# Attention and soft mixture of experts on one core: the attention output is no longer formed

## The chip, the cores and the metric

One core of a Trainium2 chip runs the whole program. The metric is device time in microseconds, from 2 runs of the kernel before.

## The reference

Attention with pooled keys comes first, then a soft mixture of experts over its output. Values are the keys. There are 4 batches of 12288 queries and 768 keys of 128 channels, and 32 slots (8 experts with 4 each).

```
kv_pool = kv.reshape(B, H // r, r, W // r, r, C).mean(axis=(2, 4))
k = v = kv_pool.reshape(B, -1, C) @ w_sr
s = scale * (q @ k.transpose(0, 2, 1))
a = np.exp(s - s.max(-1, keepdims=True))
x = ((a / a.sum(-1, keepdims=True)) @ v).reshape(B * N, C)
logits = x @ phi
d = softmax of logits over all queries (axis 0)
slot_input = d.T @ x
slot_out = for each expert: relu(slot_input @ w1) @ w2
c = softmax of logits over the slots (axis 1)
return c @ slot_out
```

The softmax over axis 0 spans all 49152 queries, so no output can be written before the last query's logits are known.

## The kernel before

All work is declared as steps for a planner (class Plan) that keeps a clock for each engine, knows a cost for each step and which buffers are free, and emits the instructions of PE, VectorE, ScalarE and GpSimd in the order that it finds. Priorities come from due times (T0 = HEAD + i * PER for block i).

The unit is a block of 512 queries (96 blocks). Scores are kept with the keys on the partitions: `qk` (L473 to L475) makes three products of 512 columns for each of 6 key tiles, with q and the keys split into a high and a low part. The maximum over the keys lies across partitions, so it takes several steps: `rowmax1` (L480) reduces with a transpose in 32x32 blocks, `rowmax2` and `rowmax_pe` (L500) bring the partition quarters together through PE, `rowmax4` (L510) transposes back and spreads it. `sub` (L518) takes the maximum from the scores on VectorE, `exp_hi` and `exp_t` (L525, L529) compute the exponential twice on ScalarE, and `plo` (L534) makes the low part of P on GpSimd.

`av_hi` and `av_lo` (L551, L552, L559) form the attention output: P is the stationary side, the values with a column of ones and the projected values (161 columns) stream, 72 products in a block. So output, sum and logits of 128 queries come out together. Every four blocks a group (`g0` to `g7a`) normalises the logits, keeps a running maximum over the queries, and adds D.T @ x to `acc` (L690: 16 fp32 products of 32 output columns in four column positions of the array).

After the last group come the slot inputs (`t_psi`, L1020), the experts (L1040, L1063), and the output: `o_mm` (L1120) multiplies the combine weights, in four row positions of the array, with the slot outputs; ScalarE and VectorE evict (L1127, L1129), SyncE's queue writes. At the head the keys of batch 0 are summed on VectorE as they land (L309 to L313), first 512 of the 768 keys and then the rest; later batches are summed by DMA.

PSUM is divided in advance: three pairs of banks for scores, two single banks for all else.

Of the kernel before, what the change touches and what calls it, by code (L numbers as in the profile page):

```python
# [11 lines left out]
F16 = mybir.dt.float16  # L12
U32 = mybir.dt.uint32
# [6 lines left out]
P = 128  # L20
EPS = 1e-9
PK = 16.0
KSPLIT = 512
VK = 4096.0
Q32 = 32


AVD = 2.0
HOLD = 0.7
URGE = 60.0  # L30


class Plan:
# [4 lines left out]

    LAG = 0.08

    def __init__(self, rings):
        self.cap = rings
        self.ops = []
        self.users = {}
        self.bank = 0

    def op(self, eng, cost, lat, prio, deps, fn, acq=(), use=(), at=0.0, slack=0.0, hot=False, raw=0.0):
        n = len(self.ops)
        if eng != "PE" and any(ring == "m" for ring, _ in use):
            prio -= URGE  # L50
        for key in list(acq) + list(use):
            self.users.setdefault(key, []).append(n)
        self.ops.append((eng, cost, lat, prio, list(deps), fn, list(acq), at, slack, hot, raw, list(use)))
        return n

    def emit(self):
        ops = self.ops
        inf = math.inf
        done = [None] * len(ops)
# [7 lines left out]
        for n, o in enumerate(ops):  # L67
            avail.setdefault(o[0], [])
            if waits[n] == 0:
                ready[n] = o[7]  # L70
                avail[o[0]].append(n)
        left = {key: len(u) for key, u in self.users.items()}
        sums = {key: sum(ops[n][0] == "PE" for n in u) for key, u in self.users.items()}
        summed = {}
# [3 lines left out]
        banks = [None] * self.cap["m"]  # L78
        tops = [None] * self.cap["m"]
        where = {}  # L80
        free = dict.fromkeys(avail, 0.0)
        todo = len(ops)

# [3 lines left out]
        def bank(key):  # L87
            found = []
            for b in range(len(banks)):
                if key[0] == "pq":  # L90
                    t = gone(banks[b])
                    beside = banks[b] is not None and banks[b][1][0] == "px" and t == inf
                    if beside:
                        t = summed.get(banks[b], inf)
                    found.append((max(t, gone(tops[b])), not beside, b))
                else:
                    found.append((max(gone(banks[b]), gone(tops[b])), False, b))
            return min(found)

        def acquire(n, now):  # L100
            t = 0.0
            for key in ops[n][6]:
                ring = key[0]
                if ring == "m":
                    t = max(t, bank(key[1])[0])
                    continue
                cap = self.cap.get(ring)
                held = rings.get(ring, ())
                if cap is not None and len(held) >= cap:
                    t = max(t, gone(held[-cap]))  # L110
            if ops[n][0] == "ACT":
                for key in ops[n][11]:
                    if key[0] == "m" and key[1][0] == "px":
                        t = max(t, gone(tops[where[key]]))
            return None if t == inf else t

        def best(e):
            found = []
            for n in avail[e]:
                t = acquire(n, free[e])  # L120
                if t is not None:
                    found.append((max(free[e], ready[n], t), ops[n][3], n))
            if not found:
                return None
            t0 = min(found)[0] + 0.12
            hot = [f for f in found if ops[f[2]][9]]
            if hot:
                h = min(hot)
                if h[0] - t0 < HOLD:
                    fits = [(p, t, n) for t, p, n in found if t <= t0 and t + ops[n][1] <= h[0] + 0.1]  # L130
                    return min(fits) if fits else (h[1], h[0], h[2])
            return min((p, t, n) for t, p, n in found if t <= t0)

        while todo:
            picks = [(c[1], e, c[2]) for e in avail if (c := best(e)) is not None]
            if not picks:
                held = {k: left[k] for k in left if left[k] and left[k] < len(self.users[k])}
# [1097 lines left out]
```

## Time and profile before

| | us |
|---|---|
| median of 2 runs | 1114.07 (1114.04 to 1114.10) |
| span of the profiled execution | 1112.4 |
| PE busy | 1046.7 (94%) |
| VectorE busy | 984.9 (89%) |
| GpSimd busy | 866.2 (78%) |
| ScalarE busy | 822.7 (74%) |

The profile is of one execution, and its span runs from the first to the last instruction; 1.7 us lie between it and the median. Matmuls are pipelined, so busy time of PE counts the time in which a product drains, and a group's mean duration is longer than the step from one product to the next. The granted clock of PE averages 0.975 of full speed.

### The profile page before, as it was taken

How to read it: one execution, taken by the hardware profiler on the slowest of the kernel's cores; microseconds unless marked ns; L12 is line 12 of the kernel's file. 1: busy time of each engine (PE TensorE's matmuls, PEld its weight loads, DVE VectorE, ACT ScalarE, POOL GpSimd, SP SyncE). 2: the span in 40 equal slices, each digit the busy share in tenths (PEclk: the TensorE clock that was granted, in tenths of full speed). 3: DMA queues.
4: the chain of work that ended last, by engine and by line, in shares of the span. 5: the costliest groups of instructions: out<-in, count | busy, mean ns of one | idle time of the engine just before them, and what ended most of it. 6: DMA issues, size and time to landing. Idle time of an engine off the chain costs nothing.

```text
span 1112.4 us, 24632 instructions
## 1 busy us (share of the span) xinstructions
PE 1046.7 (94%) x10198; PEld 897.3 (81%) x10198; DVE 984.9 (89%) x1492; ACT 822.7 (74%) x1006; POOL 866.2 (78%) x480
## 2 busy tenths in 40 slices
PE   3699999999999999999999999999999999997876
PEld 2588888888888888888888888888888888886343
DVE  7899889889889989899899988989989988987895
ACT  1677778778778778878877788688788777875563
POOL 0579897788899888789889889779889889773340
PEclk9799999999999999999999999999999999999885
DMA  9315421111125310120136210120110110113398
GB/s 342 117 22 132 96 44 39 39 58 39 39 54 124 91 42 22 39 70 27 39 83 123 71 53 1 39 96 2 39 39 1 39 39 2 39 39 115 141 407 360
DMA packets 17407, 89.15 MB, mean 80 GB/s; under 512 B 1680, under 2 KB 3984, under 8 KB 11152
## 3 DMA queue, kind: packets, MB, share of 16 engines
q1 hardware_dynamic: 13408, 69.47, 16.8%
q0 software_dynamic: 3312, 17.70, 8.4%
q8 instruction: 81, 1.33, 0.5%
q10 hardware_dynamic: 576, 0.41, 0.1%
q14 instruction: 30, 0.25, 0.1%
HBM read 58.87 MB, written 25.17 MB: 76 GB/s over the span
## 4 chain that ended last, share of the span: by engine, by line
PE 67%; DVE 27%; issue 2%; ACT 2%; POOL 1%; DMA 1%; SPq 0%; DVEq 0%; ACTq 0%; POOLq 0%
PE m L551 11%; PE m L552 10%; PE m L559 10%; PE s L473 9%; PE s L475 9%; PE s L474 9%; DVE t L518 8%; DVE r L480 8%; PE m L500 3%; PE m L690 2%; DVE mb L510 2%; PE po L1120 2%; DVE o L1129 2%; DVE cm L628 1%; DVE pool L311 1%
## 5 line engine op out<-in xcount | busy, mean ns | idle before, releaser
L534 POOL TENSOR_TENSOR plo<-t,phi 128x1536 f16<-128x1536 f32 x190 | 595.8, 3143 | 125.1 <-ACT t L529 123.8
L525 ACT ACTIVATE phi<-t,lnk 128x1536 f16<-128x1536 f32 x192 | 301.6, 1571 | 133.5 <-DVE t L518 132.9
L480 DVE TRANSPOSE_TENSOR_REDUCE r<-s 128x32 f32<-128x1024 f32 x288 | 349.8, 1236 | 27.1 <-PE s L475 21.1
L551 PE MATMUL m<-vhi,phi 128*128 128x161 f16 x2280 | 354.5, 234 | 2.5 <-DVE m L505 1.3
L552 PE MATMUL m<-vlo,phi 128*128 128x160 f16 x2280 | 353.5, 233 | 0.0
L518 DVE TENSOR_TENSOR t<-s,mb 128x1024 f32<-128x1024 f32 (+1 forms) x384 | 342.9, 949 | 8.8 <-DVE mb L510 0.9
L529 ACT ACTIVATE t<-t,lnk 128x1536 f32<-128x1536 f32 x192 | 299.8, 1568 | 2.3
L551 PEld LDWEIGHTS <-phi 128*128 128x128 f16 x2304 | 227.0, 99 | 22.9 <-issue 22.8
L473 PE MATMUL s<-qhi,khi 128*128 128x512 f32 x576 | 238.1, 413 | 6.5 <-DVE t L518 6.1
L552 PEld LDWEIGHTS <-phi 128*128 128x128 f16 x2304 | 225.5, 98 | 5.2 <-issue 3.3
L475 PE MATMUL s<-qhi,klo 128*128 128x512 f32 x576 | 227.2, 394 | 0.0
L474 PE MATMUL s<-qlo,khi 128*128 128x512 f32 x576 | 226.6, 393 | 0.0
L559 PE MATMUL m<-vhi,plo 128*128 128x161 f16 x2280 | 221.9, 233 | 0.3 <-POOL plo L534 0.3
L559 PEld LDWEIGHTS <-plo 128*128 128x128 f16 x2304 | 174.8, 100 | 1.3 <-issue 0.6
L463 POOL TENSOR_TENSOR qlo<-q,qhi 128x512 fp32r<-128x512 f32 x96 | 125.7, 1310 | 26.9 <-ACT qhi L459 26.9
L569 ACT ACTIVATE xl<-m 128x322 f32<-128x322 f32 x189 | 81.0, 428 | 76.1 <-PE m L559 75.7
L473 PEld LDWEIGHTS s<-qhi,khi 128*128 128x128 f32 x576 | 109.7, 190 | 29.9 <-issue 3.6
L475 PEld LDWEIGHTS s<-qhi,klo 128*128 128x128 f32 x576 | 109.2, 190 | 24.6 <-DVE klo L353 0.5
L474 PEld LDWEIGHTS s<-qlo,khi 128*128 128x128 f32 x576 | 109.8, 191 | 20.3 <-issue 0.7
L510 DVE STREAM_TRANSPOSE mb<-m 128x512 f32<-128x512 f32 x96 | 68.3, 711 | 3.3
L459 ACT ACTIVATE qhi<-q 128x512 fp32r<-128x512 f32 x96 | 59.2, 617 | 2.4 <-issue 1.0
L505 DVE TENSOR_REDUCE m<-m 128x16 f32<-128x64 f32 x96 | 21.5, 224 | 40.5 <-PE m L500 40.5
(140 smaller groups left out, 854.1 us busy)
## 6 DMA issues: line engine op xcount, KB each, us to landing
q<-qT SPq DMA_DIRECT2D x23, 1024.0 KB, 4.8
outT<-o SPq DMA_DIRECT2D x21, 1024.0 KB, 5.2
kva<-kvT POOLq DMA_DIRECT2D x9, 1536.0 KB, 11.4
kva<-kvT SPq DMA_DIRECT2D x3, 1536.0 KB, 10.5
kv<-kv SPq DMA_DIRECT2D x8, 512.0 KB, 5.7
w<-w SPq DMA_DIRECT2D x2, 1536.0 KB, 6.4
w<-w SPq DMA_DIRECT2D x4, 768.0 KB, 4.6
outT<-o SPq DMA_DIRECT2D x6, 512.0 KB, 4.3
```

Source lines behind the costliest of these rows:

```text
L463: nc.gpsimd.tensor_tensor(out=lo, in0=q_src(i), in1=hi.bitcast(F32), op=ALU.subtract)
L473: nc.tensor.matmul(s, khi[:, ks], hi, start=True, stop=False)
L474: nc.tensor.matmul(s, khi[:, ks], lo, start=False, stop=False)
L475: nc.tensor.matmul(s, klo[:, ks], hi, start=False, stop=True)
L480: nc.vector.tensor_reduce(out=MX[i][:, 2 * u : 2 * u + 2, :].rearrange("p t b -> p (t b)"), in_=S[i, u].rearrange("p t (b j) -> p (t b) j" ...
L518: nc.vector.tensor_tensor(out=TT_[i, h][:, o : o + n, :], in0=S[i, t // 2][:, u : u + n, :], in1=MX[i].unsqueeze(1).broadcast_to([P, n, BQ ...
L525: nc.scalar.activation(hi, TT_[i, h], AF.Exp, bias=lnk, scale=SCALE)
L529: nc.scalar.activation(t, t, AF.Exp, bias=lnk, scale=SCALE)
L534: eng.tensor_tensor(out=lo, in0=TT_.pop((i, h)), in1=PP[i, h], op=ALU.subtract)
L551: nc.tensor.matmul(px, p, vhi[:, t, :], start=(t == 0), stop=False)
L552: nc.tensor.matmul(px[:, 1:], p, vlo[:, t, :], start=False, stop=False)
L559: nc.tensor.matmul(px, PP[i, t // TH][1][:, t % TH, ks], vhi[:, t, :], start=False, stop=(t == NT - 1))
```

## The change

The program is written anew around another order of the same algebra. Its unit is a tile of 128 queries (384 tiles), its group eight tiles (48 groups).

- Scores have the queries on the partitions: `qk` multiplies a tile's q, as the stationary side, with all keys, six products of 384 columns into one slot of two PSUM banks. `rowmax` is then one reduction along a row, and `exp` one ScalarE instruction from PSUM with the maximum as its bias and the row's sum as a second result. P stays fp32.
- `turn` transposes P of two tiles in 32x32 blocks on VectorE. Keys then lie within each partition quarter, with 24 key blocks apart.
- `kv_u_mm` and `kv_u_out` multiply the pooled keys with w_sr @ phi. `l_mm` makes the logits as turned P times that: 96 fp32 products of 32 rows, 32 output columns and 256 columns for a group, in 16 positions of the array, into four banks. `l_ev`, `l_sum` and `l_turn` fold the 16 parts together.
- The attention output is not formed. `a_mm` multiplies D with P (32 slots by 768 keys), `a_ev`, `a_sc` and `a_add` keep that sum through a batch, and only at a batch's end `b_t` and `b_mm` multiply it with the values.
- PSUM is four slots of two banks, handed out by the planner to whatever step asks. The planner now picks by earliest start plus a weight times a due time from a table (DUE). Half of the combine weights (3.1 MB) are written to memory and read back at the end (`k_out`, `c_load`).
- The keys of batch 0 come in one piece of 768. The output goes out in chunks of three quads of tiles instead of four.

```diff
--- before.py
+++ after.py
-AVD = 2.0
-HOLD = 0.7
-URGE = 60.0
+NSLOT = 4
+DUE = {
...
         def best(e):
             found = []
             for n in avail[e]:
-                t = acquire(n, free[e])
-                if t is not None:
-                    found.append((max(free[e], ready[n], t), ops[n][3], n))
-            if not found:
-                return None
-            t0 = min(found)[0] + 0.12
-            hot = [f for f in found if ops[f[2]][9]]
-            if hot:
-                h = min(hot)
-                if h[0] - t0 < HOLD:
-                    fits = [(p, t, n) for t, p, n in found if t <= t0 and t + ops[n][1] <= h[0] + 0.1]
-                    return min(fits) if fits else (h[1], h[0], h[2])
-            return min((p, t, n) for t, p, n in found if t <= t0)
+                t = acquire(n)
+                if t < inf:
+                    t = max(free[e], ready[n], t)
+                    found.append((t + self.PULL * ops[n][3], t, n))
+            return min(found) if found else None
 
         while todo:
...
+    slot = [pm.tile([P, 2, 512], F32, tag=f"s{k}", name=f"s{k}") for k in range(NSLOT)]
...
+    def kv_u_mm(b):
+        for h in range(2):
+            nc.tensor.matmul(sl("pu", b)[:, h, :HK], wu_sb, pooled[b][:, h * HK : (h + 1) * HK], start=True, stop=True)
+
+    def kv_u_out(b):
+        U4[b] = bp.tile([P, NBL, NS], F32, tag="u4", name=f"u4_{b}")
+        nc.vector.transpose(out=halves(U4[b].rearrange("p b s -> p (b s)")), in_=sl("pu", b)[:, :, :HK])
...
-    def qk(i, t):
-        khi, klo = kT[i // BPB]
-        hi, lo = qsp[i]
-        if t % 2 == 0:
-            S[i, t // 2] = ps.tile([P, 2, BQ], F32, tag=f"s{t // 2}", name=f"s_{i}_{t // 2}")
-        s = S[i, t // 2][:, t % 2, :]
-        ks = slice(t * P, (t + 1) * P)
-        nc.tensor.matmul(s, khi[:, ks], hi, start=True, stop=False)
-        nc.tensor.matmul(s, khi[:, ks], lo, start=False, stop=False)
-        nc.tensor.matmul(s, klo[:, ks], hi, start=False, stop=True)
-
-    def rowmax1(i, u):
+    def qk(n):
+        khi, klo = kT[n // TPB]
+        i, o = divmod(n, TB)
+        hi, lo = (a[:, o * P : (o + 1) * P] for a in qsp[i])
+        s = sl("S", n)
+        for k, (a, b) in enumerate(((hi, khi), (hi, klo), (lo, khi))):
+            for h in range(2):
+                nc.tensor.matmul(s[:, h, :HK], a, b[:, h * HK : (h + 1) * HK], start=(k == 0), stop=(k == 2))
+
+    def rowmax(n):
+        g, o = divmod(n, GT)
+        if o == 0:
+            NM[g] = gp.tile([P, GT], F32, tag="nm", name=f"nm_{g}", bufs=3)
+            RS[g] = gp.tile([P, GT], F32, tag="rs", name=f"rs_{g}", bufs=4)
+        nc.vector.tensor_reduce(out=NM[g][:, o : o + 1], in_=sl("S", n)[:, :, :HK], axis=XY, op=ALU.max, negate=True)
+
+    def exp(n):
+        g, o = divmod(n, GT)
+        if n % 2 == 0:
+            PB[n // 2] = pp.tile([P, 2, NK], F32, tag="P", name=f"P_{n // 2}", bufs=PR)
+        nc.scalar.activation(
+            halves(PB[n // 2][:, n % 2, :]), sl("S", n)[:, :, :HK], AF.Exp, bias=NM[g][:, o : o + 1], accum_out=RS[g][:, o : o + 1]
+        )
+
+    def turn(m):
+        g, o = divmod(2 * m, GT)
+        if o == 0:
+            PT[g] = pp.tile([P, NBL, GT, Q32], F32, tag="PT", name=f"PT_{g}", bufs=2)
+        nc.vector.transpose(
+            out=PT[g][:, :, o : o + 2, :].rearrange("p b t j -> p t b j"), in_=PB[m].rearrange("p t (b j) -> p t b j", j=Q32)
+        )
+
+
+    def l_mm(g):
...
+    def l_mm(g):
+        two = [sl("L", g, 0), sl("L", g, 1)]
+        u = U4[g // GPB]
+        for b in range(NBL):
+            c = b % NQD
+            for r in range(NQD):
+                rows = slice(r * Q32, (r + 1) * Q32)
+                nc.tensor.matmul(
+                    two[r // 2][c * NS : (c + 1) * NS, r % 2, : GT * Q32], u[rows, b, :],
+                    PT[g][rows, b, :, :].rearrange("p t j -> p (t j)"), start=(b < NQD), stop=(b >= NBL - NQD),
+                )
+
...
-    def rowmax2(i):
-        top = banks[plan.bank][:, 512 - (NQD + 1) * NBK :]
...
-    def rowmax_pe(i):
-        pqv = PQ.pop(i)
-        nc.tensor.matmul(pqv, sel, MX[i].rearrange("p k b -> p (k b)"), start=True, stop=True)
-        MX[i] = pqv
...
-    def rowmax4(i):
-        m = sp.tile([P, BQ], F32, tag="mb", name=f"mb_{i}", bufs=1)
-        nc.vector.transpose(out=m, in_=MX[i].unsqueeze(2).broadcast_to([P, NBK, Q32]))
...
-    def sub(i, t, n):
...
-    def exp_hi(i, h):
-        hi = PP[i, h] = sp.tile([P, TH, BQ], F16, tag="phi", name=f"phi_{i}_{h}", bufs=PB)
-        nc.scalar.activation(hi, TT_[i, h], AF.Exp, bias=lnk, scale=SCALE)
...
-    def exp_t(i, h):
-        t = TT_[i, h]
-        nc.scalar.activation(t, t, AF.Exp, bias=lnk, scale=SCALE)
...
-    def plo(i, h):
-        lo = sp.tile([P, TH, BQ], F16, tag="plo", name=f"plo_{i}_{h}", bufs=PB)
-        eng = nc.vector if i == NB - 1 else nc.gpsimd
-        eng.tensor_tensor(out=lo, in0=TT_.pop((i, h)), in1=PP[i, h], op=ALU.subtract)
-        PP[i, h] = (PP[i, h], lo)
...
-    def av_hi(i, k):
-        _, vhi, vlo = VU[i // BPB]
-        px = av_tile(i, k)
-        ks = slice(k * P, (k + 1) * P)
-        for t in range(NT):
-            p = PP[i, t // TH][0][:, t % TH, ks]
-            nc.tensor.matmul(px, p, vhi[:, t, :], start=(t == 0), stop=False)
-            nc.tensor.matmul(px[:, 1:], p, vlo[:, t, :], start=False, stop=False)
-
...
-    def av_lo(i, k):
-        vhi = VU[i // BPB][1]
-        px = PX[i, k // 2][:, k % 2, :]
-        ks = slice(k * P, (k + 1) * P)
-        for t in range(NT):
-            nc.tensor.matmul(px, PP[i, t // TH][1][:, t % TH, ks], vhi[:, t, :], start=False, stop=(t == NT - 1))
-
...
+    def l_sum(g):
+        for r in range(NQD):
+            nc.tensor.matmul(sl("x", g)[r * NS : (r + 1) * NS, 0, : GT * Q32], sel1, G[g]["LT"][:, r, :], start=True, stop=True)
+
+    def l_turn(g):
+        lq = G[g]["lq"] = gp.tile([P, GT, NS], F32, tag="lq", name=f"lq_{g}")
+        nc.vector.transpose(out=lq.rearrange("p t j -> p (t j)"), in_=sl("x", g)[:, 0, : GT * Q32])
...
+    def a_mm(g):
+        pd = sl("A", g)
+        d = G[g]["D"]
+        for k0 in range(0, GT, NQD):
+            for h in range(2):
+                for k in range(k0, k0 + NQD):
+                    c = k % NQD
+                    nc.tensor.matmul(
+                        pd[c * NS : (c + 1) * NS, h, :HK], d[:, k, :], PB[(g * GT + k) // 2][:, k % 2, h * HK : (h + 1) * HK],
+                        start=(k < NQD), stop=(k >= GT - NQD),
+                    )
+
+    def a_ev(g):
+        if g % GPB:
+            t = G[g]["ae"] = gp.tile([P, NK], F32, tag="ae", name=f"ae_{g}", bufs=1)
+        else:
+            t = acc
+        nc.scalar.activation(halves(t), sl("A", g)[:, :, :HK], AF.Copy)
+
+    def a_sc(g):
+        nc.scalar.activation(acc, acc, AF.Copy, scale=G[g]["al"])
+
+    def a_add(g):
+        nc.gpsimd.tensor_tensor(out=acc, in0=acc, in1=G[g]["ae"], op=ALU.add)
+
+    def b_t(b):
+        for k in range(NT):
+            nc.tensor.matmul(sl("bt", b)[:, 0, k * NS : (k + 1) * NS], acc[:, k * P : (k + 1) * P], sel1, start=True, stop=True)
+
+    def b_te(b):
+        AT[b] = gp.tile([P, NT, NS], F32, tag="at", name=f"at_{b}", bufs=1)
+        nc.scalar.activation(AT[b].rearrange("p k s -> p (k s)"), sl("bt", b)[:, 0, : NT * NS], AF.Copy)
+
+    def b_mm(b):
+        for k in range(NQD):
+            ks = [j for j in range(NT) if j % NQD == k]
+            for j in ks:
+                nc.tensor.matmul(
+                    sl("bx", b)[k * NS : (k + 1) * NS, 0, :VW], AT[b][:, j, :], V[b][:, j, :], start=(j == ks[0]), stop=(j == ks[-1])
+                )
+
+    def b_x(b):
+        px = sl("bx", b)[:, 0, :VW]
+        if b == 0:
+            nc.vector.tensor_copy(xacc, px)
+        else:
+            nc.vector.tensor_tensor(out=xacc, in0=xacc, in1=px, op=ALU.add)
```

PE in the steady stage. Before, the end of one block's value products, the maximum's product, and a group's update (m is a PSUM bank, rq the maxima, xl the evicted outputs):

```order
L551 LDWEIGHTS phi_1_11842
L551 MATMUL m_113<-vhi_10049,phi_1_11842 128x161
L552 LDWEIGHTS phi_1_11842
L552 MATMUL m_113<-vlo_10050,phi_1_11842 128x160
L500 MATMUL m_112<-rq_12018,sel 128x64
L559 LDWEIGHTS plo_0_11836
L559 MATMUL m_113<-vhi_10049,plo_0_11836 128x161
...
L690 MATMUL m_112<-xl_11205,D_11952 32x129 x16
```

PE now, from one tile's scores to the next tile's across a group's update and logits (s is a PSUM slot, P and PT the exponentials and the turned ones, u the projected keys):

```order
L353 MATMUL s_104<-khi_1894,qhi_2928 128x384 x2
L353 MATMUL s_104<-klo_1895,qhi_2928 128x384 x2
L353 MATMUL s_104<-khi_1894,qlo_2929 128x384 x2
L490 MATMUL s_101<-P_2649,D_3118 32x384 x2
...
L490 MATMUL s_101<-P_2858,D_3118 32x384 x2
L386 MATMUL s_102<-PT_3034,u_1_2088 32x256 x2
L386 MATMUL s_103<-PT_3034,u_1_2088 32x256 x2
...
L353 MATMUL s_104<-khi_1894,qhi_3141 128x384 x2
```

The value products have gone. A group's update stands directly ahead of another group's logits, and with them three of the four slots are taken between two tiles' scores.

VectorE in the steady stage. Before, one block from its first reduction to its last subtraction (r, m and mb are stages of the maximum, t the scores less it):

```order
L480 TENSOR_REDUCE r_50_7124<-s_0_7107 128x32
L480 TENSOR_REDUCE r_50_7124<-s_1_7119 128x32
L606 RECIPROCAL r_7155<-xl_6647 128x16
L480 TENSOR_REDUCE r_50_7124<-s_2_7130 128x32
L490 TENSOR_REDUCE m_112<-r_50_7124 128x16
L492 TENSOR_TENSOR rq_7180<-m_112,quad 128x64
L505 TENSOR_REDUCE m_50_7193<-m_112 128x16
L510 STREAM_TRANSPOSE mb_7195<-m_50_7193 128x512
L518 TENSOR_TENSOR t_0_7216<-s_0_7107,mb_7195 128x1024
```

VectorE now, a stretch of a group (nm is the maxima, lq and cm stages of the logits, klo the next batch's keys):

```order
L413 RECIPROCAL rs_4352<-rs_4352 128x8
L360 TENSOR_REDUCE nm_4595<-s_103 128x1
L402 STREAM_TRANSPOSE lq_4795<-s_104 128x256
L360 TENSOR_REDUCE nm_4595<-s_101 128x1
L429 TENSOR_REDUCE cm_4806<-ll_4798 128x8
...
L360 TENSOR_REDUCE nm_4835<-s_104 128x1
L374 STREAM_TRANSPOSE PT_4755<-P_4821 128x2x24x32
L478 TENSOR_REDUCE al_4899<-da_4840 128x1
L533 TENSOR_REDUCE RM<-ll_4556 128x8
L360 TENSOR_REDUCE nm_4835<-s_102 128x1
L374 STREAM_TRANSPOSE PT_5002<-P_4851 128x2x24x32
L374 STREAM_TRANSPOSE PT_5002<-P_4889 128x2x24x32
```

A tile leaves VectorE one maximum and half a turn; the subtractions and the stages of the maximum are gone, and the group's small steps stand between them.

## Rows read from the trace of the kernel before

**Rows 1.** Busy time by stage: length, busy us of each engine (records), granted clock, DMA share, GB/s.

```profile
120.00:900.00 780.00, 770.60 (x7697) 679.09 (x7696) 706.14 (x1044) 614.23 (x734) 674.81 (x364) 1.00 0.19 50
...
1042.00:1112.40 70.40, 49.42 (x382) 28.45 (x381) 54.95 (x87) 39.88 (x66) 18.75 (x19) 0.75 0.88 358
```

**Rows 2.** Groups by form, PE, 120 to 900 us: xcount, busy us, mean ns, idle before.

```profile
L500 PE MATMUL m<-rq,sel 128*128 128x64 f32 x152 | 31.8, 290 | 7.1 <-DVE rq L492 6.6
...
L690 PE MATMUL m<-xl,D 128*32 128x129 f32 x608 | 20.7, 275 | 0.0
```

**Rows 3.** Timeline, PE, about 400 to 406 us: start, length, line, operation, count.

```profile
400.32 0.58 PE L559 MATMUL m<-vhi,plo 128*128 128x161 f16 x6
400.89 1.09 PE L690 MATMUL m<-xl,D 128*32 128x129 f32 x32
401.91 0.24 PE L551 MATMUL m<-vhi,phi 128*128 128x161 f16 x1
...
405.17 0.39 PE L473 MATMUL s<-qhi,khi 128*128 128x512 f32 x1
405.40 0.39 PE L474 MATMUL s<-qlo,khi 128*128 128x512 f32 x1
```

**Rows 4.** Timeline, PE, 400.85 to 400.99 us alone.

```profile
400.89 0.32 PE L690 MATMUL m<-xl,D 128*32 128x129 f32 x4
```

**Rows 5.** Timeline, PE, in the tail.

```profile
1037.18 2.78 PE L1063 MATMUL pso<-w,hT 128*32 128x512 f32 x24
...
1045.24 0.50 PE L1120 MATMUL po<-chi,shi 32*128 32x512 f32 x4 [0.53 <-ACT o L1127]
1045.57 0.40 PE L1120 MATMUL po<-clo,shi 32*128 32x512 f32 x4
```

**Rows 6.** Groups by form, whole run.

```profile
L480 DVE TRANSPOSE_TENSOR_REDUCE r<-s 128x32 f32<-128x1024 f32 x288 | 349.8, 1236 | 27.1 <-PE s L475 21.1
...
L518 DVE TENSOR_TENSOR t<-s,mb 128x1024 f32<-128x1024 f32 x192 | 233.9, 1218 | 8.8 <-DVE mb L510 0.9
...
L518 DVE TENSOR_TENSOR t<-s,mb 128x512 f32<-128x512 f32 x192 | 122.7, 680 | 0.0
...
L510 DVE STREAM_TRANSPOSE mb<-m 128x512 f32<-128x512 f32 x96 | 68.3, 711 | 3.3
...
L715 DVE TENSOR_REDUCE RM<-LL 128x16 f32<-128x512 f32 x23 | 14.5, 651 | 0.0
...
L1063 PE MATMUL pso<-w,hT 128*32 128x512 f32 x32 | 3.8, 598 | 0.0
```

**Rows 7.** Timeline, VectorE, a block's subtractions and maxima in the tail.

```profile
412.38 3.55 DVE L518 TENSOR_TENSOR t<-s,mb 128x1024 f32<-128x1024 f32 x4
...
1028.09 1.86 DVE L715 TENSOR_REDUCE RM<-LL 128x16 f32<-128x512 f32 x3
```

**Rows 8.** Groups by form, ScalarE and GpSimd, whole run.

```profile
L525 ACT ACTIVATE phi<-t,lnk 128x1536 f16<-128x1536 f32 x192 | 301.6, 1571 | 133.5 <-DVE t L518 132.9
...
L1127 ACT ACTIVATE o<-po 128x1024 f32<-128x1024 f32 x23 | 23.6, 1025 | 19.1 <-PE po L1120 10.9 <-issue 5.5 <-ACT RM L720 1.6
...
L463 POOL TENSOR_TENSOR qlo<-q,qhi 128x512 fp32r<-128x512 f32 x96 | 125.7, 1310 | 26.9 <-ACT qhi L459 26.9
```

**Rows 9.** Timeline of the head, PE and VectorE.

```profile
17.85 2.08 PE L344 MATMUL m<-pooled,w_sb 128*128 128x512 f32 x2 [8.92 <-DVE pooled L313]
...
21.12 0.83 PE L473 MATMUL s<-qhi,khi 128*128 128x512 f32 x1
...
24.09 0.42 DVE L313 TENSOR_TENSOR pooled<-pool 128x256 f32<-128x256 f32 x1
```

**Rows 10.** Timeline of the tail, PE: last scores, slot inputs, first output.

```profile
1000.72 0.39 PE L475 MATMUL s<-qhi,klo 128*128 128x512 f32 x1
...
1026.42 0.64 PE L1020 MATMUL m<-sel,acc 128*128 128x32 f32 x2 [0.61 <-DVE acc L696]
...
1042.94 0.71 PE L1120 MATMUL po<-chi,shi 32*128 32x512 f32 x4
```

More of the change, by code (lines that the diff above doesn't have):

```diff
@@ L69, in emit @@
             if waits[n] == 0:
-                ready[n] = o[7]
+                ready[n] = o[8]
                 avail[o[0]].append(n)
         left = {key: len(u) for key, u in self.users.items()}
-        sums = {key: sum(ops[n][0] == "PE" for n in u) for key, u in self.users.items()}
-        summed = {}
         part = {}
@@ L77, in emit, with acquire @@
         rings = {}
-        banks = [None] * self.cap["m"]
-        tops = [None] * self.cap["m"]
-        where = {}
+        slots = [None] * NSLOT
         free = dict.fromkeys(avail, 0.0)
         todo = len(ops)
+        self.log = []
         def gone(key):
             return 0.0 if key is None else freed.get(key, inf)
[L87 to L100, printed above, removed]
+        def acquire(n):
             t = 0.0
+            need = [key for key in ops[n][6] if key[0] == "s"]
+            if need:
+                t = sorted(gone(s) for s in slots)[len(need) - 1]
             for key in ops[n][6]:
                 ring = key[0]
-                if ring == "m":
-                    t = max(t, bank(key[1])[0])
+                if ring == "s":
                     continue
-                cap = self.cap.get(ring)
+                cap = self.cap[ring]
                 held = rings.get(ring, ())
-                if cap is not None and len(held) >= cap:
+                if len(held) >= cap:
                     t = max(t, gone(held[-cap]))
[L111 to L115, printed above, removed]
+            return t
         def best(e):
@@ L136, in emit @@
             if not picks:
[L137 to L138 removed]
+                raise RuntimeError("the plan is stuck: " + str([(e, [(ops[n][3], ops[n][6]) for n in avail[e]][:8]) for e in avail]))
             t, e, n = min(picks)
[L140 removed]
+            eng, cost, lat, due, deps, fn, acq, use = ops[n][:8]
             avail[e].remove(n)
             free[e] = t + cost
[L143 removed]
+            end = t + cost + lat
             todo -= 1
             for key in acq:
[L146 to L149 removed]
+                if key[0] == "s":
+                    k = min(range(NSLOT), key=lambda i: (gone(slots[i]), i))
+                    slots[k] = key
+                    self.where[key] = k
                 else:
                     rings.setdefault(key[0], []).append(key)
[L152 removed]
+            for key in acq + use:
                 left[key] -= 1
                 part[key] = max(part.get(key, 0.0), end)
[L155 to L158 removed]
                 if left[key] == 0:
```

1050 lines of the change are left out of this document (369 added, 681 removed), and 4 rows, old and new, of the table DUE.

## The prediction

> **What bounds the kernel now.** I read the stage table first. From 120 to 900 us PE is busy 770.6 of 780.0 us, VectorE 706.1, GpSimd 674.8, ScalarE 614.2 [rows 1], and what PE still waits for in that stage is 6.6 us for the operand of the maximum's product [rows 2]. So PE sets the pace there, and an engine that is merely relieved gains nothing. The maximum's product leaves two records for each block of 512 queries; 152 of them are 76 blocks [rows 2], so a block takes 780/76 = 10.26 us, and 1024 queries take 20.5.
>
> The second reading is how much of that is product work. A key product of 512 columns starts 0.23 us after the one before it, and six value products take 0.58 us of which the last one's own 0.23 is drain, so 0.07 each [rows 3]. A block has 18 of the first (4.14), 72 of the second (5.04), the maximum's product (0.27) and a quarter of a state update of 1.09 (0.27): 9.72, with the next batch's keys 9.9. That is 96.5% of 10.26. The rest is drain and short waits that the busy share hides. I use this 96.5% below as what a bound engine reaches under a planned order.
>
> **PE after the change, for a group of eight tiles (1024 queries).** Key products: 48 of 384 columns. At 0.23 for 512, a column costs 0.45 ns, so 0.172 each, 8.3 us. The value products (10 us for as many queries) and the product for the maximum go.
>
> The logits (L386) are 96 fp32 products of 256 columns with 32 rows and 32 output columns. An fp32 product runs as two records: 16 calls of L690 leave 32 [rows 3]. Do positions run side by side? Four records of L690, in the four column positions, take 0.32 us, where one alone takes 0.27 [rows 2, 4]. All 32 take 1.09, so a round of four takes (1.09-0.32)/7 = 0.11 for 129 columns. L1063's 24 records, one of which takes 0.60, are six rounds in 2.78, (2.78-0.60)/5 = 0.436 for 512 columns [rows 5, 6]. Both are 0.85 ns for a column and a record. The four row positions appear in L1120: four records start as one, take 0.50, and the next four begin 0.33 later [rows 5]. Columns alone and rows alone are therefore shown; all 16 positions at once are not. If they combine, 192 records are 12 rounds of 256 x 0.85 = 0.217, or 2.6 us. If rows queue behind one another, it is 48 rounds, 10.4. I take 2.6: rows and columns each showed no loss, and L1120's four products together already fill the array and write four banks.
>
> The update with P (L490) has 32 records of 384 columns in column positions: 8 rounds of 0.326, 2.6 us. The folding (L398) is two rounds, 0.43; the small maximum product 0.27. A change of position costs time: the last L559 starts at 400.67 and L690 only at 400.89, 0.15 more than the usual step, and 401.91 is 0.14 later than a ninth round would be [rows 3]. Three such runs in a group make 0.9. Sum 8.3 + 2.6 + 2.6 + 0.43 + 0.27 + 0.9 = 15.1 us; 48 groups 725, and the keys of four batches about 12: **PE 737 us**.
>
> **VectorE.** Four subtractions take 3.55 us while their durations add to 3.80, so successive instructions overlap by 0.08 [rows 6, 7]. Three maxima of 512 take 1.86: (1.86-0.65)/2 = 0.605 a step; the step for 1024 in the subtractions is 1.14. So 1.05 ns an element, and a maximum over 768 costs 0.87. Eight make 7.0. The transpose of 512 lasts 711 ns, step 0.63 [rows 6]; the turn has 1536 elements: 0.63 + 1024 x 1.05 = 1.70. Its strided write of 32-element pieces isn't shown; the dearest rate of a row that works across 32 partitions is L480's, 1236 ns for 1024, so 1.70 to 1.85, and I take 1.70, as the operation is the same as L510's. Four make 6.8. The small ones (transpose of 256: 0.36, the column maximum 0.35, the row maximum 0.34, and six of some 0.15) make 2.0. Sum 15.8; 48 groups 758, keys 7: **VectorE 765 us**. Subtraction, the second pass of the maximum and its copies are gone, but the turn takes their place.
>
> **The covered engines.** ScalarE's exponential reads 768 from PSUM: L1127's 1025 ns less 256 elements gives 0.81; bias and running sum are in no row together with PSUM. Between 0.81 and the 1.57 of a whole 1536 [rows 8] I take 0.95, near the first. Eight make 7.6, with the splits of q, the evictions and the rescaling about 12.5 a group; at 1.57 it would be 17.5 and bind (840 us). GpSimd: two remainders of q at 1.31 [rows 8], the sum of 768 about 1.6, small ones 3: 7.2. Both lie under VectorE's 15.8 at nothing.
>
> **The ends.** Today the first key product starts at 21.12, 3.3 us after the first part of the keys was pooled (17.85), while the last was pooled at 24.5 [rows 9]. The new code waits for the whole batch: 24.5 + 3.5 = 28. From the last key product to the slot inputs: maximum, exponential and turn 3.7, logits with eviction, folding and turn 5.2, softmax chain 4.5, update 2.9, eviction and sum 2.4, the two short products and hops 5.3: 24 (today 25.7, from 1000.72 to 1026.42 [rows 10]). From there to the end today 1112.4 - 1026.4 = 86.0, of which the last 70.4 move the output at 358 GB/s [rows 1]; same bytes, same products, so 86. The logits that were parked in memory come back there, with the weights 9.9 MB, 28 us at that rate: just covered by the drain of 24 and the four before it; uncovered up to 10.
>
> **The sum.** VectorE is the later engine: 765/0.965 = 793. 28 + 793 + 24 + 86 = 931 of span, and 1114.07 - 1112.4 = 1.7 around it (the median stands that much above the profiled span): **933 us**.
>
> **Rivals.** First, the logits' records come slower than the array takes them. L690's 32 records are 1.09 us for 32, (1.09-0.27)/31 = 26 ns each, and no longer row of this kernel is denser. If 26 ns is the pace at which records are handed over, 192 need 5.0 us, not 2.6: PE 737 + 115 = 852, over 0.965 883, **1023 us**. For it: a group now issues 384 instructions for these products. Against: within a round of four the starts lie within 0.05 us (0.32 less 0.27) [rows 4], so single handovers are quicker. [...]
>
> Second, the four PSUM slots. The update holds one and the logits two, some 4 us with the evictions, and leave one of four for scores. A slot is held about 3.3 us for a tile (product 1.0, maximum 0.95, exponential 0.95, hops), so one slot feeds 1.3 tiles where 2.1 are due: 1.6 us lost a group, 77 in all, **1010 us**. Against: the order puts two turns and up to three maxima of finished scores there, 5 to 6 us of VectorE work.
>
> Third, on the other side: row positions wait for each other when column positions are in use too, and the change doesn't do what it says. Logits 10.4 us: PE 737 + 375 = 1112, over 0.965 1152, with the ends 1291, **slower**. It decides from 6.9 us for the logits of a group on (PE 941, 975 with drains, 1114 in all).
>
> **How the numbers follow.** Forecast 0.63 (893 to 975), pace of records 0.20, slots 0.09, queueing rows 0.06, other 0.02. Low end: VectorE without a gap, 765 + 28 + 24 + 80 = 899, less a short overlap, 893. High end: the rival at 1023, which also takes in the dearer turn (+29) and the uncovered loads (+10). Two per cent, 22 us, is what can be told from no change: faster 0.90, within 0.04, slower 0.06.
>
> **What would show it.** First key product (L353) near 28; then 16.5 us a group, VectorE busy over 95% in the steady stage and PE about 93%; the 192 records of one L386 run within 2.6 to 2.9 us; the output stage at some 360 GB/s. Wrong: runs of L386 over 4 us; a turn above 1.9 us; an exponential above 1.3; a granted clock under the 1.00 of the steady stage [rows 1], since PE has only 4% to spare.

## The result and the profile after

The changed kernel takes **1042.45 us** (median of 2 runs, 1042.38 to 1042.51) against 1114.07: a ratio of 0.936, 95% interval 0.933 to 0.938. It is faster, but by 72 us where 181 were forecast, and 1042 lies above the range (893 to 1023). The profiled execution has a span of 1040.6 us.

The stage table of the kernel after (columns as in [rows 1], of which these are the counterparts):

```profile
120.00:900.00 780.00, 723.78 (x11999) 542.56 (x12000) 666.21 (x895) 539.88 (x1181) 318.20 (x395) 1.00 0.22 56
975.00:1040.60 65.60, 47.90 (x412) 31.14 (x404) 50.48 (x97) 37.66 (x76) 16.77 (x21) 0.70 0.85 346
```

In the steady stage PE is busy 723.8 of 780 us, the 93% that were forecast, but VectorE 666.2, 85% where over 95% was expected. So VectorE waits for PE; what PE itself waits for stands in PE's groups of the same stretch (after the bar: busy us, mean ns, then idle time before and its cause):

```profile
L353 PE MATMUL s<-khi,qhi 128*128 128x384 f32 x676 | 189.1, 361 | 18.3 <-ACT P L366 18.1 <-issue 0.2
L386 PE MATMUL s<-PT,u 32*32 32x256 f32 x8064 | 179.3, 385 | 34.8 <-issue 24.3 <-DVE al L478 9.8 <-ACT acc L500 0.5
...
L490 PE MATMUL s<-P,D 128*32 128x384 f32 x1352 | 117.9, 489 | 0.0
```

L386 are the logits. 24.3 us of PE's idle time lie ahead of them with the cause "issue": nothing that the profile shows was missing. The 18.1 us ahead of L353 are waits for a PSUM slot that an exponential frees. The groups of the whole run answer to [rows 6, 8]:

```profile
L366 ACT ACTIVATE P<-s,nm 128x768 f32<-128x768 f32 x384 | 343.5, 897 | 149.9 <-DVE nm L360 149.4
L360 DVE TENSOR_REDUCE nm<-s 128x1 f32<-128x768 f32 x384 | 354.2, 943 | 85.0 <-PE s L353 84.0
L374 DVE STREAM_TRANSPOSE PT<-P 128x1536 f32<-128x1536 f32 x192 | 334.7, 1756 | 0.0
...
L366 ACT ACTIVATION_READ_ACCUMULATOR P<-s,nm 128x1 f32 x384 | 74.5, 194 | 0.0
```

Maximum and turn have the forecast sizes (0.943 and 1.756 us). Nearly all of VectorE's idle time ahead of the maxima, 84.0 us, is waiting for key products: PE is the bound. The timeline of PE shows why, in two runs of the same 192 logits records (start, length, count, idle time before):

```profile
125.47 3.28 PE L386 MATMUL s<-PT,u 32*32 32x256 f32 x148 [0.29 <-DVE al L478]
131.21 1.33 PE L386 MATMUL s<-PT,u 32*32 32x256 f32 x44 [2.47 <-issue]
...
162.97 4.01 PE L386 MATMUL s<-PT,u 32*32 32x256 f32 x192 [0.29 <-DVE al L478]
```

The second is an undisturbed run: 4.01 us where 2.6 were forecast, and none of the 48 runs is under 4.00. The first stops once in its middle and takes 7.07 us. A stop, below, is a wait of over 0.4 us between two starts of one run: 28 of the 48 runs have one, 44 us together. The transfers between 128.80 and 129.95, inside the first run's stop, hold one packet of code:

```profile
q8 instruction: 1, 0.02, 5.5%
```

By its size, and by its 36 packets fewer with half the products (below), queue q8 (`instruction` in the profile) moves PE's code: 112 packets of 16 KB in the run (81 before), 1.84 MB for 14284 weight loads and as many records, so some 64 bytes an instruction and 256 in a packet. The packets lie 9 us apart in the mean, and by the trace's transfer records **all 28 stops end 1.25 to 1.57 us after the end of a q8 packet**.

The ends. The first key product starts where it was forecast (28; PE's timeline, answers to [rows 9]), but the way from the last key product (ends at 912.4) to the slot inputs (L724), the drain of the kernel, takes 35.7 us, not 24 (answers to [rows 10]). The row at 402.93 is an update of the steady stage:

```profile
27.90 0.85 PE L353 MATMUL s<-khi,qhi 128*128 128x384 f32 x2
...
402.93 2.79 PE L490 MATMUL s<-P,D 128*32 128x384 f32 x32
...
916.45 5.34 PE L490 MATMUL s<-P,D 128*32 128x384 f32 x32 [3.18 <-POOL D L471]
921.73 3.62 PE L386 MATMUL s<-PT,u 32*32 32x256 f32 x156
927.31 1.23 PE L386 MATMUL s<-PT,u 32*32 32x256 f32 x36 [1.96 <-issue]
...
936.01 4.42 PE L490 MATMUL s<-P,D 128*32 128x384 f32 x32 [2.76 <-POOL D L471]
...
948.08 0.63 PE L724 MATMUL s<-sel,xacc 128*128 128x32 f32 x2 [0.51 <-DVE xacc L529]
```

An update (L490) that takes 2.79 us in the steady stage takes 5.34 and 4.42 here. The windows of the drain (granted clock third from the end) show 0.50 where the first of them ran, after PE had stood still for 3.2 us; in the second one's window the mean is 0.66:

```profile
900.00:912.00 12.00, 11.34 (x255) 7.62 (x248) 9.92 (x14) 7.63 (x16) 3.90 (x4) 1.00 0.35 124
...
916.40:921.70 5.30, 5.25 (x32) 1.38 (x32) 2.21 (x4) 0.94 (x1) 1.40 (x3) 0.50 0.93 349
...
936.00:941.00 5.00, 4.42 (x32) 1.31 (x32) 0.19 (x1) 1.37 (x2) 0.74 (x2) 0.66 0.15 60
```

**Where the 109.6 us went** (1040.6 against a forecast span of 931): key products 27.9 to 912.4, 884.5 in place of 793 (18.4 us a group, not 16.5), +91.5; drain +11.7, of which the last group's logits (921.73 to 928.54, 6.8 us with a stop, in place of 2.6) make 4.2; slot inputs to the end, 92.5 in place of 86, +6.5; start 0.

### The profile page after: what moved, and what is told of

It is laid out like the page before. It is cut to its first block, busy times and chain, and to the rows that moved or that the text cites. A ratio compares the mean times of both kernels' runs of the same rounds, so it can differ in the third digit from the quotient of the medians.

```text
span 1040.6 us, 32723 instructions
## 1 busy us (share of the span) xinstructions
PE 910.6 (88%) x14284; PEld 667.8 (64%) x14284; DVE 843.8 (81%) x1181; ACT 665.7 (64%) x1447; POOL 390.1 (37%) x485
## 3 DMA queue, kind: packets, MB, share of 16 engines
q8 instruction: 112, 1.84, 0.7%
## 5 line engine op out<-in xcount | busy, mean ns | idle before, releaser
L366 ACT ACTIVATE P<-s,nm 128x768 f32<-128x768 f32 x384 | 343.5, 897 | 149.9 <-DVE nm L360 149.4
L360 DVE TENSOR_REDUCE nm<-s 128x1 f32<-128x768 f32 x384 | 354.2, 943 | 85.0 <-PE s L353 84.0
L374 DVE STREAM_TRANSPOSE PT<-P 128x1536 f32<-128x1536 f32 x192 | 334.7, 1756 | 0.0
L386 PE MATMUL s<-PT,u 32*32 32x256 f32 x9216 | 206.5, 387 | 46.8 <-issue 33.4
L353 PE MATMUL s<-khi,qhi 128*128 128x384 f32 x768 | 215.3, 362 | 21.9 <-ACT P L366 21.7
L386 PEld LDWEIGHTS s<-PT,u 32*32 32x32 f32 x9216 | 138.1, 103 | 120.6 <-issue 48.5
L353 PE MATMUL s<-khi,qlo 128*128 128x384 f32 x768 | 196.9, 338 | 0.1
L353 PE MATMUL s<-klo,qhi 128*128 128x384 f32 x768 | 196.8, 338 | 0.0
L353 PEld LDWEIGHTS s<-khi,qhi 128*128 128x128 f32 x768 | 131.0, 190 | 71.3 <-issue 39.6
L490 PE MATMUL s<-P,D 128*32 128x384 f32 x1536 | 138.0, 501 | 5.9 <-POOL D L471 5.9
L353 PEld LDWEIGHTS s<-klo,qhi 128*128 128x128 f32 x768 | 139.9, 189 | 0.3 <-issue 0.3
L353 PEld LDWEIGHTS s<-khi,qlo 128*128 128x128 f32 x768 | 139.6, 189 | 0.5 <-POOL qlo L343 0.5
L490 PEld LDWEIGHTS s<-P,D 128*32 128x32 f32 x1536 | 45.9, 112 | 75.7 <-issue 68.9
```

What stands on the lines that cost most here:

```text
L353: nc.tensor.matmul(s[:, h, :HK], a, b[:, h * HK : (h + 1) * HK], start=(k == 0), stop=(k == 2))
L360: nc.vector.tensor_reduce(out=NM[g][:, o : o + 1], in_=sl("S", n)[:, :, :HK], axis=XY, op=ALU.max, negate=True)
L366: nc.scalar.activation(halves(PB[n // 2][:, n % 2, :]), sl("S", n)[:, :, :HK], AF.Exp, bias=NM[g][:, o : o + 1], accum_out=RS[g][:, o : o + 1]
L374: nc.vector.transpose(out=PT[g][:, :, o : o + 2, :].rearrange("p b t j -> p t b j"), in_=PB[m].rearrange("p t (b j) -> p t b j", j=Q32))
L386: nc.tensor.matmul(two[r // 2][c * NS : (c + 1) * NS, r % 2, : GT * Q32], u[rows, b, :], PT[g][rows, b, :, :].rearrange("p t j -> p (t j)" ...
L490: nc.tensor.matmul(pd[c * NS : (c + 1) * NS, h, :HK], d[:, k, :], PB[(g * GT + k) // 2][:, k % 2, h * HK : (h + 1) * HK], start=(k < NQD), ...
```

## The experiments

Two theories of the logits at the start: A, the 384 instructions of a group's logits reach the array too slowly, and their code too late; B, sixteen positions gain less than sixteen-fold on columns. Rival C: VectorE, the slots or the order set the pace, and the logits matter little. All ratios are against the kernel before, with 95% intervals; the changed kernel has 0.936 (0.933 to 0.938).

### Half the columns

```diff
-  two[r // 2][c * NS : (c + 1) * NS, r % 2, : GT * Q32], u[rows, b, :],
-  PT[g][rows, b, :, :].rearrange("p t j -> p (t j)"), ...
+  two[r // 2][c * NS : (c + 1) * NS, r % 2, : GT * Q32 // 2], u[rows, b, :],
+  PT[g][rows, b, : GT // 2, :].rearrange("p t j -> p (t j)"), ...
```

> Each logits product takes 128 columns in place of 256 (the logits of half of the queries are left out, the eviction writes the other half twice); the instructions stay as many. Theory A, instructions: L386's 384 instructions reach the array at 8.3 ns each after the first 64, and their code comes late in some runs. Then a run keeps its length, median 3.8 to 4.0 us with the same single gaps of 0.5 to 2.9 us, and the time stays at 1030 to 1043 us. Theory B, array: sixteen positions gain less than sixteen-fold on the columns. Then a run halves to about 2.0 us, the group falls from 18.5 to 16.5 us and the time to some 946 (1042 less 48 x 2.0).

991.5 us, ratio 0.890 (0.888 to 0.892). PE's timeline, one undisturbed run:

```profile
168.77 2.74 PE L386 MATMUL s<-PT,u 32*32 32x128 f32 x192
```

Neither number came: 2.74 us, not 3.9 and not 2.0. A price per instruction alone is wrong, since columns count; columns alone are wrong too. The starts of single records in these runs show the pattern (ns from a run's first record; the trace doesn't name a record's product, it is read off the order and the 215 ns of a pass in one position):

```
changed kernel, 256 columns: rounds start at 622, 1268, 1916   648 ns and 34 records (17 products) apart
half the columns, 128:       rounds start at 436,  870, 1303   434 ns and 34 records (17 products) apart
changed kernel:   1st product ends at 587; 17th product starts at 430, 18th at 622
                  18th product ends at 1233; 35th product starts at 1268
half the columns: 1st product's first pass ends at 293, its second at 401; 17th product starts at 319, 18th at 436
```

128 columns fewer in each of two passes take off 214 ns, 0.84 ns a column as forecast; **220 ns of each round remain whatever the columns**: five times in a run of 96 products, 1.1 us. The 18th product starts 35 ns after the end of the first, drain and all as the profile models it, and the 35th 35 ns after the end of the 18th. Neither pair shares a position or a PSUM address. The 17th, which does share its position with the first, starts before the first has ended (430 against 587). So seventeen products are on their way, not one for each position. A product is four instructions (two weight loads, two passes): 64 places that come free in the program's order give just this, as the 17th's first pass then needs only the first product's first pass to have ended (293, 26 ns ahead of its start at 319), and the 18th's needs its second. 21 of the 48 runs still stop for code (49 us), since the instructions are as many.

### Half the products

```diff
-        for b in range(NBL):
+        for b in range(NBL // 2):
```

> Half of the logits products (the second half of the keys is left out of the logits): 96 records, 192 instructions, 256 columns each. Theory A, instructions: 96 records fewer at 16.6 ns take 1.6 to 1.7 us off a run, so 4.0 becomes 2.3 to 2.4; a run now holds less than the 256 instructions of one 16 KB packet of code, so the gaps nearly go as well and the mean falls from 4.8 to about 2.5. The group then stands on VectorE, 15.6/0.965 = 16.2 us, and the time is 930 to 950 us. Theory B, array: 2.0 us, gaps unchanged, some 960. Theory C, PSUM slots or the order hold VectorE up: it keeps most of its 84 us of waits and the time stays above 1000 us.

909.1 us, ratio 0.817 (0.816 to 0.818), below what any theory gave. PE's timeline of one run, and the window of its steady stage:

```profile
171.97 2.12 PE L386 MATMUL s<-PT,u 32*32 32x256 f32 x96
```

```profile
120.00:780.00 660.00, 621.85 (x7890) 467.80 (x7889) 644.96 (x877) 525.35 (x1158) 312.78 (x382) 1.00 0.24 63
```

All 48 runs take 2.11 to 2.13 us and **none stops for code**; q8 has 76 packets, 36 fewer for 9216 instructions fewer, which is 256 in each. VectorE is now busy 645 of 660 us, 98%. Most groups take 15.5 us, the mean of all is 15.8: a little faster than the 16.5 that the prediction wanted from it. C is refuted as a cause apart from the logits: with them short, and their slots free sooner, slots and order let VectorE run full.

### Half the turn

```diff
-  out=PT[g][:, :, o : o + 2, :]..., in_=PB[m].rearrange(...)
+  out=PT[g][:, :, o : o + 1, :]..., in_=PB[m][:, :1, :].rearrange(...)
```

> VectorE turns only one tile of each pair, and the logits products read that one twice (the logits of every second tile are left out): PE has the same 192 records and columns, VectorE about 3.3 us a group less (15.6 to 12.3). If PE with its logits sets the pace (A or B): the time stays within 1020 to 1043 us, and VectorE's waits for L353 grow from 84 to some 230 us. If VectorE sets the pace, as the prediction had it: the group falls by up to 2 us and the time below 990 us.

1029.2 us, ratio 0.925 (0.922 to 0.927). VectorE is relieved by 148 us of work (843.8 to 696.0) and the time falls by 13; its waits for L353 grow from 84 to 172 us (230 expected). The steady window shows VectorE at 69% and PE at 94%: VectorE is not the bound.

```profile
120.00:900.00 780.00, 733.02 (x12213) 547.49 (x12206) 538.51 (x899) 535.62 (x1188) 318.05 (x392) 0.99 0.22 57
```

### The planner's costs

```diff
-        lm = op("PE", 2.75, 0.17,
+        lm = op("PE", 4.6, 0.17,
...
-    PER = 1.95
+    PER = 2.2
```

> Same work and instructions, another order: the planner is told 4.6 us for the logits in place of 2.75, 2.9 for the update, 1.09 for the exponential, 1.84 for the state's sum, and 2.2 us a tile. Theory A: what an order can give back are PE's waits for the exponential and the scale, 18 + 10 us in 780, so 1015 to 1043 us, and L386's runs keep their 4.0 us and their gaps. Theory C, the order made for the wrong costs is what costs the time: VectorE's waits for L353 fall by more than half and the time falls under 1000 us.

1050.5 us, ratio 0.943 (0.942 to 0.945): 8 us longer, outside A's numbers too, and why isn't shown. VectorE's waits for L353 fell (84.0 to 47.7 us, not the half that C wanted), and so did PE's waits for a slot (21.7 to 4.9 us in the whole run; total, times, longest):

```profile
PE s L353 <- ACT P L366: 4.9, 5, 1.2
```

The time didn't fall with them, so neither this order nor the slots are what costs it. The stops for code remain (35 us).

### What the next round waits for: address, position or number

```diff
-  two[r // 2][c * NS : (c + 1) * NS, r % 2, : GT * Q32], u[rows, b, :],
+  two[r // 2][c * NS : (c + 1) * NS, r % 2, (b // NQD % 2) * GT * Q32 :][:, : GT * Q32], u[rows, b, :],
```

> Successive products of one position write the two halves of their PSUM bank in turn (the second half is not evicted, so half of the keys are left out of the logits); positions, order, columns and instructions stay. In the trace of the changed kernel a product starts 35 ns after the full end of the product sixteen before it, the last one in its position: a round of sixteen lasts 648 ns, 428 of columns and 220 more. If that wait is for the PSUM address that both write, the 220 go: a run falls from 4.0 to 2.7 us and the time by some 1.3 x 48 = 60 us, to 980. If it belongs to the position, or to sixteen products on their way at once, a run stays 4.0 us and the time 1030 to 1045 us.

1046.9 us, ratio 0.940 (0.938 to 0.941), undisturbed runs still 4.00 us: not the address. (This expectation and the next count sixteen products, the last one in the same position. By the count above it is seventeen, and the product that is waited for stands in another position.)

```diff
-        for b in range(NBL):
+        for r0, b in ((r0, b) for r0 in (0, 2) for b in range(NBL)):
...
-            for r in range(NQD):
+            for r in range(r0, r0 + 2):
```

> The same products, but first all of two row positions, then all of the other two, so eight positions at a time. A position then has six products behind one another twice, 12 x 0.428 = 5.1 us of columns. If sixteen products can be on their way at once and the seventeenth waits for the first to end, eight positions never reach that: a run takes 5.1 to 5.4 us, with fewer gaps of late code, 1040 to 1075 us. If a position takes its next product only when its last has drained, 12 x 0.648 = 7.8 us, some 1042 + 3 x 48 = 1190 us, slower than before. If the pace of instructions alone decided, a run would keep 4.0 us.

1086.3 us, ratio 0.976 (0.973 to 0.979), above the 1040 to 1075 expected, but the run has the expected length. PE's timeline:

```profile
177.09 5.24 PE L386 MATMUL s<-PT,u 32*32 32x256 f32 x192 [0.28 <-DVE al L478]
```

5.24 us is 24 passes in a position at 0.216: with eight positions no product waits for another's end: a position's second product starts at 430 ns, while its first ends at 587. So not the position; it is the number on their way at once. There are 16 stops for code (28 in the changed kernel), 20 us in all.

### Logits in parts

The logits are issued as two (or three) steps, with a wait of 1 us in the plan between them, in which it puts key products. The plan also takes 4.2 us for the logits, and lets the second exponential of a pair wait for the first.

```diff
+        for z in range(NP):
+            lm = [op("PE", 4.2 / NP, 0.17, ("lm", t0), lm, lambda z=z: l_mm(g, z * NBL // NP, (z + 1) * NBL // NP),
+                     acq=LK if z == 0 else [], use=[("PT", g), ("u", b)] + (LK if z else []), raw=1.0)]
```

> All work done; a group's logits products are issued in two parts of 48 with at least one tile's key products between (and the planner's cost for them is 4.2 us in place of 2.75). If the gaps come from code that is read too late for 384 instructions in one piece, as half of the products showed, parts of 192 instructions lose nearly all of them: 0.8 us a group, less some 0.3 for one more change of position, so 0.5 x 48 = 24 us, 1010 to 1025 us. If the gaps follow the amount of code (a packet of 256 instructions, 2.2 a group), they move elsewhere and the time stays at 1035 to 1050 us.

> The same in three parts of 32 products. One more change of position and two PSUM slots held 1 us longer: if late code is the cause and the slots are not short, 1010 to 1030 us; if the slots bind, VectorE's waits for L353 grow and it is over 1045 us.

Two parts: **1035.6 us**, ratio 0.930 (0.929 to 0.931). Three: 1083.1, ratio 0.972 (0.969 to 0.974). The first time lies where gaps that follow the amount of code would put it, but the stops tell: with two parts, and the same 112 packets of code, they fall from 44 to 11 us (7 stops), so they follow the length of the dense piece. In the changed kernel they were 24.3 us of PE's waits; now, in the waits of 120 to 900 us (total, times, longest), and with PE's busy time of the same stretch:

```profile
PE s L386 <- issue: 2.2, 2, 1.9
```

```profile
120.00:900.00 780.00, 750.06 (x12111) 527.63 (x12109) 677.82 (x902) 547.77 (x1187) 317.67 (x393) 1.00 0.21 55
```

Yet 7 us are won, not 17 to 32, and PE is busy 96% in place of 93. By the starts of the records, a group spends 0.84 us less inside the logits, but 0.44 more where one kind of product follows another (1.6 such changes more), 0.20 more between its key products and 0.09 more inside the small product of the maximum (L439); the expectation had 0.3 for all of this. What the stops alone cost is therefore not shown in time.

With three parts VectorE waits 107 us for L353. That the slots, held longer, bind there isn't shown: PE's waits for a slot in the whole run are 26.0 us (21.7 in the changed kernel), while the changes between kinds of products take 1.12 us a group more, 0.45 of it waiting.

```profile
PE s L353 <- ACT P L366: 26.0, 41, 1.7
```

### The drain kept busy

```diff
+    for key, n, dep in (("a", 18, ops["qk", NTL - 1]), ("b", 12, ops["ls", NG - 1]), ("c", 15, ops["g3m", NG - 1]), ("d", 15, ops["am", NG - 1])):
+        op("PE", 0.173 * n, 0.17, T(NTL), [dep], fill(key, n), acq=[("s", "f", key)], use=[("k", B - 1), ("qs", NTL // TB - 1)])
```

> The changed kernel with 60 idle products (key products of the last tile into free PSUM slots, read by nobody) where PE stands still behind the last tile; the planner then also puts the last logits ahead of the update before. In the trace of the changed kernel PE stands for 3.2 us at 912.9, the granted clock is 0.50 from 916.4 to 921.7 and 0.51 to 0.66 from 929 to 948, and the two updates take 5.3 and 4.4 us there in place of 2.8. If the standing still is what costs the clock, the updates take 2.8 us again, the way from the last key product to the slot inputs falls from 35.7 to 28 to 30 us and the time to 1034 to 1037 us. If the clock stays low there, or the products only stand in the way, 1040 to 1046 us.

> The same with the logits in two parts, as in the experiment with two parts, which gained 7 us. If the two gains have different causes they add: 1026 to 1031 us. If the gain of the parts was the order of the drain alone, 1033 to 1037 us, as with the filling only.

Filled: 1037.3 us, ratio 0.930 (0.927 to 0.934), at the edge of what was expected; the interval touches that of the changed kernel, so the drain's own length is the better evidence. PE's timeline (L682 are the idle products) and windows of the drain:

```profile
925.92 2.79 PE L490 MATMUL s<-P,D 128*32 128x384 f32 x32
...
933.77 2.87 PE L682 MATMUL s<-khi,qhi 128*128 128x384 f32 x15
936.68 2.79 PE L490 MATMUL s<-P,D 128*32 128x384 f32 x32
```

```profile
920.50:926.00 5.50, 5.42 (x196) 4.17 (x200) 0.75 (x3) 1.23 (x2) 1.66 (x4) 0.69 0.39 159
...
936.00:941.00 5.00, 4.95 (x45) 2.85 (x44) 0.19 (x1) 2.39 (x5) 1.91 (x4) 1.00 1.00 411
```

Both updates take 2.79 us again and the way to the slot inputs 30.7 us (28 to 30 expected). Where PE still stood for 2.5 us, ahead of the last logits, the clock fell all the same (0.69). Both edits together: **1027.7 us, ratio 0.923 (0.921 to 0.925)**, drain 28.3 us: the gains add (15 us, of 7 and 5), and this beats the changed kernel with all of its arithmetic kept.

### One pass in place of two

```diff
-  u[rows, b, :], PT[g][rows, b, :, :].rearrange("p t j -> p (t j)"), ...
+  u[rows, b, :].bitcast(BF16)[:, 1::2], PT[g][rows, b, :, :].rearrange("p t j -> p (t j)").bitcast(BF16)[:, 1::2], ...
```

> The logits products read only the upper halves of the words of P and U, as bf16, so the logits have 8 bits of each factor; all 96 products stay, each now one weight load and one record, 192 instructions in place of 384, in one pass of 0.107 us in place of two. If the limit found is sixteen products on their way at once, a round lasts 0.107 + 0.16 + 0.035 = 0.30 us and a run 6 x 0.30 + 0.1 = 1.9 us. If it is 64 instructions, 32 products may be on their way, two for each position, nothing drains between rounds, and a run takes 0.8 to 1.3 us. In both cases gaps of late code are nearly gone (192 instructions in one piece) and VectorE binds as with half of the products: 900 to 915 us. Above 950 us something else than the logits would set the pace.

**916.4 us, ratio 0.824 (0.822 to 0.826)**, just above the 900 to 915 expected. PE's timeline and the steady window:

```profile
172.57 1.16 PE L387 MATMUL s<-PT,u 32*32 32x256 bf16 x96
```

```profile
120.00:780.00 660.00, 591.97 (x7759) 448.86 (x7758) 638.84 (x871) 520.97 (x1149) 311.98 (x382) 0.99 0.24 63
```

1.16 us, within the 0.8 to 1.3 of "64 instructions". In the record starts of the run at 139.30 us, 32 products start within 181 ns; the 33rd follows at 316, 27 ns after the first's end (289), the 65th at 613, 26 ns after the 33rd's (587). A product is two instructions here, so 32 fill 64 places. No run stops for code, and VectorE sets the pace (97%).

## Why the prediction was wrong

**The step that failed** is the logits' term, "If they combine, 192 records are 12 rounds of 256 x 0.85 = 0.217, or 2.6 us ... I take 2.6". The 0.217 is right and the positions do combine: in a run's first round sixteen records start within 113 ns. Two things that the rows of before couldn't show were missing.

1. *On their way at once: 64 instructions.* An fp32 product is two weight loads and two records (9216 of each for 4608 products); sixteen are 64, the first pass of the seventeenth slips in when the first product's first pass has ended, and the rest waits until its second has. In bf16 a product is two instructions, and 32 fit. 4.01 - 2.6 = 1.4 us a group, 68 us: 1.1 are the five waits, the rest the spread of the starts and the last products' drain. Shown by the record starts of the changed kernel and of those with half the columns, eight positions and one pass, with address and position excluded. A place came free only at the end of its instruction, with the drain that the profile models: the 18th fp32 product starts 35 ns after the end of the first, the 33rd bf16 one 27 ns. The rows of before, L690 in [rows 3] and L1120 in [rows 5], used four positions, and the limit doesn't show even with eight (5.24 us, 24 passes of 0.216).
2. *Late code.* 384 instructions in 4 us use 1.5 packets of code, and a packet's arrival decides when a run goes on: 44 us in 28 runs. Shown by the stops' ends, and by pieces of 192 instructions, which have none or few of them with the same or less code.

PE's forecast of 737 with 68 and 44 added is 849 us, over the 96.5% used there 880, against 884.5 measured. So good a fit is in part luck: 44 is the length of the stops and not their price (the two parts took 33 us of it away and won 7), and some of the drain in the 68 stood in the prediction's changes of position already. PE's other terms held: key products 0.173 us apart (0.172 forecast), an update 2.79 with its drain (2.6 without).

**The choice of bound** fell with it. VectorE's 765 over 0.965 = 793 was the later engine only with logits under 3.2 us ((765 - 737)/48 above 2.6). Its own sizes were good (turn 1.756 us, maximum 0.943 with a step near 0.87) and a little high in sum: where it sets the pace (half the products) a group takes 15.8 us in the mean, not 16.5.

**The rivals.** The first, records that come slower than the array takes them, came true in its place and nearly in its time (1023), but not by its mechanism: not 26 ns a record, but 7.5 in the first round and then a wait for the drain (220 ns of each round). Eight positions at 5.24 us are a full eight-fold (24 passes of 0.216 in each), so what sixteen lack, 4.01 us where 2.6 were forecast, belongs to the instructions on their way, not to the positions. The second rival, slots, cost 21.7 us of PE's waits (L353 behind an exponential), not 77, and with 4.9 of that left (the planner's costs) the time was no shorter. The third, queueing row positions, is refuted: 4.0 us, far from its 6.9.

**The covered engines** held. ScalarE's exponential is 0.897 us and a separate accumulator read of 0.194, together over the 0.95 taken and under its bound; GpSimd's sum 1.84 for 1.6. Neither binds (539.9 and 318.2 of 780).

**The ends.** Start right. The drain is the second miss, +11.7 us: the prediction named a granted clock under 1.00 as what would make it wrong, but took the steady stage's 1.00 for the drain too. The filled drain took 5 us back by the clock and by its other order (last logits ahead of the update before), which weren't separated; with the parts 7.4 us. The last logits' 4.2 us belong to the step that failed. Of the 6.5 us between slot inputs and end, a part is the output's 346 GB/s in place of 360 (25.2 MB, some 3 us); the rest, and why, stays open, as it wasn't tried.

## What to carry to other kernels

Small products in many array positions were limited here by how many were on their way, not by the array alone: take the latency of one product with its drain (587 ns for an fp32 one here), multiply by the rate wanted, and count what that needs in instructions (an fp32 product is four, a bf16 one two; 64 were on their way here). A long piece of short instructions on PE also needed its code in time: 384 in one piece stopped for 44 us in the run, cut in two with longer work between for 11. But count a change of position for each cut: of the 0.84 us a group that was won inside the logits, 0.44 went to such changes and 0.29 between and inside other products. PE paid again in clock where it stood still in the drain (0.50 after 3.2 us), and idle products there, with the order that came with them, shortened the drain by 5 us.

## What the runs showed of the hardware

- In the 32x32 positions of these runs 64 instructions were on their way at once: the 18th fp32 product starts 35 ns after the first has ended, the 33rd bf16 product 27 ns (the ends are modelled by the profile).
- Within the first sixteen products, starts are 7.5 ns apart in the mean in fp32 and 3.3 in bf16; in later rounds 17 and 8. In fp32 sixteen first passes (0 to 113 ns) go ahead of the second ones (215 to 353), although the program has one product after another.
- Where PE stopped in a run of 384 instructions, it resumed 1.25 to 1.57 us after a 16 KB packet of code has landed (28 stops).
- An exponential with a running sum is two instructions, 0.897 and 0.194 us.
- After PE stood for 2.5 to 3.2 us, the granted clock of the next stretch was 0.50 to 0.69.
